# w_in in even and odd partitions, its sums moved to chunk 0, and late query blocks in a home of their own

## The chip, the cores and the metric

The kernel runs on one core of a Trainium2 chip. The metric is the device time of one execution in microseconds; the median of three runs of the kernel before is 273.5 us (273.16 to 273.62). A profiled execution is kept beside it, and every time below is from that one. The engines are PE (matrix products), DVE, ACT and POOL (element by element), and SP, which here only issues transfers (DMA) and transposes by DMA.

## The reference

An attention with a cosine weight feeds a feed-forward layer. Eight batches, eight heads, 576 positions, 64 columns a head; then 4608 tokens of width 512, and a hidden width of 2048.

```python
r = maximum(x, 0); phi(x) = concat([r * cos(theta), r * sin(theta)])     # theta = pi/2 * pos/576
kv  = einsum('bhsf,bhfd', ...)      # phi(k)^T v, one 128 x 64 matrix a head
num = phi(q) @ kv;  den = phi(q) @ sum_s phi(k) + 1e-6
x   = (num / den), heads side by side: 4608 x 512
h   = x @ w_in;  g = h * sigmoid(beta * h);  out = g @ w_out
```

## The kernel before

**Batches and chunks.** A batch has 576 positions; partition p of a head holds positions 9p to 9p+8, so a batch is nine blocks (`NQ`) of 64 positions. Two heads g = 0, 1 lie in partitions 0 to 63 and 64 to 127 of the raw tiles, and index j counts the four pairs. The feed-forward layer works in nine chunks of 512 tokens, eight blocks each, so chunk 0 is blocks 0 to 7 of batch 0, and chunk 1 is block 8 of batch 0 and blocks 0 to 6 of batch 1.

**Attention of a batch.** `load_raw` brings q, k or v (SP's queue; one buffer for each of the three). DVE and ACT take relu of k (`k_relu`, L193/L192) and v times cos and sin (`v_scale`, L219/L217; `vb`). PE multiplies both (`kv_mm`, L276), and ACT or DVE copies the result (`kv_take`, L286). The relu of q (`q_relu`, `qb`) is turned, by PE (`q_turn_pe`, L235, then copies by ACT and tangent products by DVE, L223) in batches 0 and 1, by a DMA transpose (`q_turn_dma`, L259) in the others; the sine half of q is the cosine half times tan (`tan_mul`, `qs`). PE forms the numerators (`num_mm`, L297), DVE divides (`x_rden`, `x_mul`, L308 to L319: `xs`), and `xs` is turned into `xt` by PE (`x_turn_pe`, L356, copied by ACT or DVE, L361/L363) or by DMA (`x_turn_dma`, L367).

**Feed-forward of a chunk.** `h_mm` (L386) multiplies a hidden block of 128 with w_in, `h_act` (L394) applies the silu on ACT. Chunk 0 multiplies g with w_out plainly (`o_mm`, L544). From chunk 1 on the second layer, and from chunk 3 on the first, runs with seven products of halves instead of eight; it needs sums of the operands: of g (`g_sum`, S1 to S4, L406), of x (`x_sum`), of w_in (`wh_sum`, L443, 32 instructions in all) and of w_out (`w_sums`, T1 to T4, L876 to L879).

**Weights.** `load_w` brings w_in in four column blocks and w_out in four row blocks through four stage buffers. w_in's rows come as rows 128j + p, while the attention has its features by (g, jj); so `cast_win` (L111 to L115) writes bf16 with a change of partitions, each instruction on 64 of them. `cast_out` (L121/L123) multiplies w_out by 1/beta. When the stage buffers are free, `wx_tiles` makes four homes of them: two for the sums of w_in, one for x's, one for a second `qs`.

**The order.** All is recorded by hand, engine by engine. Up to the end of chunk 0, 32 slots follow one another: 0 to 15 the hidden blocks, 16 to 31 the second layer; `early` names what is added behind a slot. `rest()` behind slot 4 records the casts of w_in and w_out and the loads of batch 1; `second()` turns q of batch 1 behind slot 23. Chunk 1 has slots 0 to 15 (`h_group`), with `num_rest` (blocks 7 and 8 of batch 1) behind slot 0, `w_sums` behind slot 6 and the kv of batch 2 behind slot 10; then the seven products of the second layer, `x` and `y`, by name ("6" is a product with S2, "cu" ACT's copy of what has come so far). From chunk 2 on `ORDERS` lists the steps of each chunk; in it `W61` is the first sum of w_in's hidden block 12, and so on.

**Start.** The first 58 small products (`warm_pe`) only keep PE busy until data lands. The table of tangents is turned by PE and copied by DVE (L694).

## Time and profile before

| | us |
|---|---|
| median of three runs (lowest, highest) | 273.5 (273.16, 273.62) |
| the profiled execution, its span | 274.44, 272.7 |
| PE, DVE, ACT, POOL busy | 265.3, 224.0, 188.4, 68.3 |
| chunk 0's first complete product group begins | 18.88 |
| second layer of chunk 0 begins | 31.77 |
| chunk 1 begins | 50.36 |
| second layer of chunk 1 begins | 65.91 |
| last matmul ends | 269.0 |

The page gives busy time, and the chain of work that ended last: 85% of the span are PE's, 9% DVE's, 3% a transfer of v. The granted clock of PE is full throughout. The 16 DMA engines are full up to about 44 us (388 GB/s between 20 and 30 us) with the loads of batches 0 and 1 and of all weights. Times of an instruction are counted from the span's start. Where PE waits is read from the table by stretches, and what it waits for from the timelines.

### The profile page before, as it was taken

What the parts mean: (1) busy time and instruction counts of PE and PEld (TensorE: products, weight loads), DVE (VectorE), ACT (ScalarE), POOL (GpSimd) and SP (SyncE); (2) the same over time, 40 slices, a digit from 0 to 9 for tenths busy, and PEclk for the clock granted to TensorE, in tenths of its full rate; (3) what the DMA queues carried; (4) which work ended last, traced back from release to release, by engine and by line L of the source; (5) the groups of instructions that cost most, each with busy time, mean ns of one, the idle gap of its engine ahead of it and who ended that gap; (6) DMA issues with size and microseconds to landing.
All of it is one profiled execution on the core that took longest, in us unless ns stands there. A gap on an engine that the chain in (4) does not pass through costs nothing.

```text
span 272.7 us, 8970 instructions
## 1 busy us (share of the span) xinstructions
PE 265.3 (97%) x3712; PEld 206.8 (76%) x3712; DVE 224.0 (82%) x596; ACT 188.4 (69%) x384; POOL 68.3 (25%) x89
## 2 busy tenths in 40 slices
PE   8899999999899999999999999999999999999994
PEld 8554455455784588888888888888888888888883
DVE  5989969499989889789989997899589768757852
ACT  4778777796419656899489966996696179428920
POOL 1444000510078000660085009300840060000001
PEclk9999999999999999999999999999999999999999
DMA  6999999999969999994589439943600570015005
GB/s 237 374 395 383 392 390 319 379 201 336 284 130 311 240 348 226 240 313 103 147 216 370 92 58 223 332 71 62 181 2 2 61 185 1 2 27 130 0 2 155
DMA packets 50681, 54.00 MB, mean 198 GB/s; under 512 B 31232, under 2 KB 31760, under 8 KB 50640
## 3 DMA queue, kind: packets, MB, share of 16 engines
q1 hardware_dynamic: 47504, 45.55, 59.1%
q0 software_dynamic: 2784, 7.61, 9.6%
q8 instruction: 29, 0.48, 0.7%
q10 hardware_dynamic: 352, 0.27, 0.4%
q14 instruction: 12, 0.10, 0.1%
HBM read 36.71 MB, written 9.44 MB: 169 GB/s over the span
## 4 chain that ended last, share of the span: by engine, by line
PE 85%; DVE 9%; DMA 3%; SPq 1%; issue 1%; ACT 1%; DVEq 0%
PE ps L621 32%; PE ps L511 27%; PE ps L386 10%; PE ps L544 5%; PE ps L563 4%; PE ps L297 3%; DMA raw_v<-in_v_dram 3%; PE ps L276 3%; DVE vb L219 1%; DVE xs L319 1%; DVE qs L223 1%; SPq L79 1%; DVE S L406 1%; DVE rk L193 1%; DVE qb L193 0%
## 5 line engine op out<-in xcount | busy, mean ns | idle before, releaser
L537 POOL DMA_DIRECT2D out_dram<-o_sb x58 | 33.9, 591 | 147.3 <-ACT o_sb L658 86.3
L420 ACT ACTIVATE g_t<-ps,beta 128x512 bf16<-128x512 f32 x96 | 60.3, 702 | 1.4 <-PE ps L511 1.3
L621 PEld LDWEIGHTS <-S 128*128 128x128 bf16 x448 | 43.4, 98 | 5.2
L511 PE MATMUL ps<-w_stage 128*128 128x256 bf16 x288 | 46.6, 272 | 0.1
L386 PE MATMUL ps<-xt,win 128*128 128x512 bf16 (+1 forms) x196 | 42.8, 375 | 0.1
L511 PEld LDWEIGHTS <-w_stage 128*128 128x128 bf16 x384 | 37.3, 98 | 5.1 <-issue 0.2
L487 DVE TENSOR_TENSOR ps<-ps,p 128x256 f32<-128x256 f32 x74 | 30.5, 428 | 8.6 <-PE ps L511 3.0
L394 ACT ACTIVATE g_t<-ps,beta 128x512 bf16<-128x512 f32 x48 | 32.3, 688 | 7.2 <-PE ps L386 7.1
L621 PEld LDWEIGHTS <-g_t 128*128 128x128 bf16 x336 | 32.3, 98 | 4.5 <-ACT g_t L420 0.4
L386 PEld LDWEIGHTS <-win 128*128 128x128 bf16 x196 | 18.7, 98 | 21.1 <-issue 0.5
L511 PE MATMUL ps<-xt,win 128*128 128x256 bf16 x192 | 32.9, 273 | 0.0
L511 PEld LDWEIGHTS <-win 128*128 128x128 bf16 x288 | 28.0, 98 | 3.4
L621 PE MATMUL ps<-wout,g_t 128*128 128x256 bf16 x224 | 28.9, 273 | 0.0
L406 DVE TENSOR_TENSOR S<-g_t 128x512 bf16<-128x512 bf16 (+1 forms) x66 | 25.7, 418 | 3.3 <-ACT g_t L420 1.7
L480 ACT COPY ps<-ps 128x256 f32<-128x256 f32 x62 | 22.6, 383 | 7.5 <-PE ps L621 4.0
L217 ACT ACTIVATE vb<-raw_v,sin 128x256 bf16<-128x256 f32 (+1 forms) x58 | 26.0, 503 | 1.5 <-DMA raw_v<-in_v_dram 1.5
L621 PE MATMUL ps<-T,S 128*128 128x256 bf16 x224 | 26.6, 273 | 0.0
L621 PE MATMUL ps<-wout,S 128*128 128x256 bf16 x224 | 26.4, 273 | 0.0
L319 DVE TENSOR_TENSOR xs<-ps,rden 128x768 bf16<-128x768 f32 (+4 forms) x26 | 22.8, 884 | 0.9 <-DVE rden L312 0.2
L223 POOL TENSOR_TENSOR qs<-qt,tanr 128x1152 bf16<-128x1152 bf16 x6 | 14.3, 2387 | 27.4 <-PE ps L563 21.0
L658 ACT COPY o_sb<-ps 128x512 f32<-128x512 f32 x11 | 6.3, 587 | 20.1 <-PE ps L621 20.1
L487 DVE TENSOR_TENSOR ps<-ps,u 128x256 f32<-128x256 f32 x36 | 15.3, 427 | 5.3 <-PE ps L511 3.3
(112 smaller groups left out, 414.7 us busy)
## 6 DMA issues: line engine op xcount, KB each, us to landing
raw_v<-in_v_dram SPq DMA_DIRECT2D x7, 1152.0 KB, 9.7
raw_k<-in_k_dram SPq DMA_DIRECT2D x7, 1152.0 KB, 9.5
raw_q<-in_q_dram SPq DMA_DIRECT2D x7, 1152.0 KB, 7.4
out_dram<-o_sb POOLq DMA_DIRECT2D x58, 128.0 KB, 4.5
w_stage<-in_moe_w_in_dram SPq DMA_DIRECT2D x3, 1024.0 KB, 12.8
w_stage<-in_moe_w_out_dram SPq DMA_DIRECT2D x2, 1024.0 KB, 7.9
w_stage<-in_moe_w_out_dram SPq DMA_DIRECT2D x4, 512.0 KB, 11.9
out_dram<-o_sb SPq DMA_DIRECT2D x10, 128.0 KB, 2.4
```

The lines of the kernel that those rows point to most:

```text
L217: got = nc.scalar.activation(o, a, AF.Copy, scale=t[:, n : n + 1])
L223: return eng.tensor_tensor(dst.rearrange("q n (g p) -> q n g p", g=2), src.rearrange("q n (g p) -> q n g p", g=2), tanr[:, n0:n1].unsqueez ...
L319: nc.vector.tensor_tensor(o.rearrange("q j n s d -> q j (n s) d"), nv[:, :, a:z, :, 0:D].rearrange("q j n s d -> q j (n s) d"), rden[:, :, ...
L386: nc.tensor.matmul(ps[:, h_bank(c, jt), i * 64 : (i + w) * 64], lhsT=win[jt // 4][:, mi, (jt % 4) * P : (jt % 4 + 1) * P], rhs=xt[:, i : i ...
L394: return nc.scalar.activation(gs[c, jt // 4][:, jt % 4], ps[:, h_bank(c, jt)], AF.Silu, scale=beta[:, jt : jt + 1])
L406: return nc.vector.tensor_tensor(o, l, r, op=op)
L420: return nc.scalar.activation(gs[c, jt // 4][:, jt % 4], bank, AF.Silu, scale=beta[:, jt : jt + 1])
L480: return nc.scalar.copy(at("a", 0), at("b", 0))
L487: nc.vector.tensor_tensor(dst, at("b", 0), st["p5"], op=ALU.add)
L511: nc.tensor.matmul(dst, lhsT=l[:, g], rhs=r[:, :, g * HP : (g + 1) * HP], start=start and g == 0, stop=g == 1, skip_group_check=True)
L537: (eng or own).dma_start(out=out_v[bb, n][:, m0:m1], in_=o_sb[hf * HP : (hf + 1) * HP, m0:m1])
L621: nc.tensor.matmul(dst, lhsT=l(i), rhs=r[:, i], start=start and i == 0, stop=i == order[-1], skip_group_check=True)
```

## The change

**w_in.** Feature column d of head 4 jj + mi now lies at 2d + jj in block mi. The raw tiles keep their pairs but `heads` gives the two heads of a product as j and j + 2; the division writes `xs` with a step of two columns; w_in's rows are loaded so that row d of jj = 0 goes to the even partitions and of jj = 1 to the odd ones, with two transfers of 64 partitions in place of each. `cast_win` then needs no change of partitions: one instruction casts 128 of them.

**Sums.** The 32 sums of w_in go to a home of their own and are taken on DVE in chunk 0 (behind the casts of each column block, and the last of them behind slots 22 and 27). All `W` steps leave `ORDERS`. T1, T2 and T4 are summed in halves, partly in chunk 0; T3 behind slot 0 of chunk 1. S1 to S4 move into two stage buffers.

**Casts.** Blocks 6 and 7 of w_out are cast on ACT, with others changed in place; w_in(0) has four casts (POOL, DVE, ACT, POOL), w_in(1) to (3) four each, all DVE.

**Queries of batch 1.** PE turns blocks 0 to 6. Blocks 7 and 8 get their relu on ACT into a piece of T1, and are turned by two DMA transposes on SP; POOL makes their tangent products. Their numerators (`num_rest`) go behind slot 11 of chunk 1, and the kv of batch 2 with them. Block 8 of batch 0 is multiplied and divided behind slot 22 in place of slot 4; its sine half is kept by a copy of POOL's (`qs_last`).

**Order.** The loads of batch 2 stand behind these transposes on SP; w_out(2) is loaded in two halves around q of batch 1; the relus of q(3) on ACT stand behind the two p copies of the second layer. In chunk 1 the first halves of four hidden blocks come first. Slots 4 to 9 split their products in two of 256 columns.

**Start.** A small read of v stands ahead of beta on ACT's queue, the copies of the table of tangents go to ACT, and four of the first products fall away.

```diff
+    def heads(j0, j1):
+        if j1 - j0 == 4:
+            return slice(0, 4)
+        at = 2 * (j0 % 2) + j0 // 2
+        return slice(at, at + 1) if j1 - j0 == 1 else slice(at, 4, 2)
...
-    w_in_v = moe_w_in.rearrange("(j p) f -> p j f", p=P)
+    late_qb = T1[:, 6:8].rearrange("q i t -> q (i t)").rearrange("q (s n c) -> q s n c", s=2, n=2)
+    w_in_v = moe_w_in.rearrange("(jj mi d) f -> jj d mi f", jj=2, d=HP)
...
-            nc.sync.dma_start(out=st[:, a : a + step], in_=w_in_v[:, a : a + step, i * 512 : (i + 1) * 512])
+            for jj in range(2):
+                nc.sync.dma_start(out=st[jj:P:2, a : a + step],
+                                  in_=w_in_v[jj, :, a : a + step, i * 512 : (i + 1) * 512])
...
+    nc.scalar.dma_start(out=touch, in_=v[0].rearrange("h (s r) d -> (h s) r d", s=2)[:, 0, 0:8])
...
-        parts = ((0, 0, 5), (1, 5, NQ))
+        parts = ((0, 0, 5), (1, 5, NQ)) if b == 0 else ((0, 0, 4), (1, 4, 7))
...
-        o = xs[:, n0:n1, jps[0] : jps[-1] + 1].rearrange("q n s (j d) -> q j n s d", j=2)
+        o = xs[:, n0:n1, jps[0] : jps[-1] + 1].rearrange("q n s (d j) -> q j n s d", j=2)
...
-        nc.vector.tensor_copy(tanr[:, n0:n1, :].rearrange("q n p -> q (n p)"), ps[:, bank, 0 : (n1 - n0) * HP])
+        nc.scalar.copy(tanr[:, n0:n1, :].rearrange("q n p -> q (n p)"), ps[:, bank, 0 : (n1 - n0) * HP])
...
+    def t_sum(kind, i0, i1):
+        o, l, r = {1: (T1, B12, B11), 2: (T2, B22, T1), 4: (T4, B21, T2), 3: (T3, B22, B12)}[kind]
+        nc.vector.tensor_tensor(o[:, i0:i1], l[:, i0:i1], r[:, i0:i1], op=ALU.subtract)
...
     def rest():
+        nc.gpsimd.tensor_copy(qs_last, qs_first[:, :, NQ - 1])
         cast_halves(2)
+        wh_sums(0)
+        wh_sums(2)
         cast_halves(3)
-        x_mul(x_rden(2, 0, 8, NQ, (0, 1)), 8, NQ)
+        wh_sums(4)
+        wh_sums(6)
...
+        load_w("out", 2, 2, 0, 2)
         load_raw(1, "q")
-        load_w("out", 2, 2)
+        load_w("out", 2, 2, 2, 4)
         load_w("out", 3, 2)
-        x_turn_dma(0, 8, 9)
-        for j in range(8):
+        for j in range(4):
             cast_out(j)
+        wh_sums(8)
+        wh_sums(10)
+        cast_out(4)
+        cast_out(5)
+
+    def rest_2():
+        cast_out(6, "a")
+        cast_out(7, "a")
+        v_scale(1, 1, n1=8, eng="act")
+        k_relu(1, 2, 4, "act")
+        t_sum(1, 0, 4)
         v_scale(1, 0)
         v_scale(1, 1, n0=8)
         k_relu(1, 0, 2)
+        t_sum(2, 0, 4)
...
+    def eighth():
+        for jp in range(2):
+            num_mm(0, 8, jp, 4, jp)
+        kv_mm(1, 0, 6)
+        kv_mm(1, 1, 6)
+        kv_take((0, 1), 6, "act")
+        x_mul(x_rden(4, 0, 8, NQ, (0, 1)), 8, NQ)
+        x_turn_dma(0, 8, NQ)
+        cast_out(8)
+        cast_out(9, "a")
+        t_sum(4, 0, 4)
+        wh_sums(12)
+        q_relu(1, 0, n1=7)
+        q_relu(1, 1, n1=4)
+        q_relu(1, 1, "act", 4, 7)
+        for jp in range(2):
+            relu(late_qb[:, jp].rearrange("q n (j d) -> q j n d", j=2), raw_tile(1, "q")[:, jp::2, 7:], "act")
+        for jp in range(2):
+            nc.sync.dma_start(out=qts[1][:, jp, 7:], in_=late_qb[:, jp].rearrange("q n c -> q (n c)"), transpose=True)
+
+    def turn():
+        for jp in range(2):
+            tan_mul(nc.gpsimd, qs_first[:, jp, 7:], qts[1][:, jp, 7:], 7, NQ)
+        load_raw(2, "q")
+        load_raw(2, "v")
+        load_raw(2, "k")
+        takes = [q_turn_pe(1, jp, 4 + 2 * jp, hold=True) for jp in range(2)]
...
+    def sevens():
+        for jp in range(2):
+            num_seven(jp, 4 + 2 * jp)
+        for j in (14, 15):
+            cast_out(j, "a")
+        for jp in range(2):
+            x_mul(x_rden(4 + 2 * jp, 0, 0, 7, (jp,)), 0, 7)
+        t_sum(1, 4, 8)
+        wh_sums(14)
...
-        4: lambda: (num_mm(0, 8, 0, 2, 0), num_mm(0, 8, 1, 2, 1), rest()),
-        15: lambda: (v_scale(1, 1, n1=8, eng="act"), k_relu(1, 2, 4, "act")),
+        4: rest,
+        15: rest_2,
+        22: eighth,
+        25: turn,
+        27: sevens,
+        30: lambda: x_turn_pe(1, 0, 7, 4, ("act",), (0,)),
+        31: lambda: (x_turn_pe(1, 0, 7, 5, ("dve",), (1,))),
...
+    t_sum(2, 4, 8)
+    t_sum(4, 4, 8)
+    for jt in range(4):
+        h_mm(1, jt, (0, 1))
     for slot in range(16):
...
-            num_rest()
             att_q(2)
             v_half(2, 0)
+            t_sum(3, 0, 8)
...
-        elif slot == 10:
+        elif slot == 11:
+            num_rest()
             kv_all(2, eng="act")
+            x_rest()
...
-    q_relu(3, 0, "act")
...
     ops(y, "1 c1")
+    q_relu(3, 0, "act")
+    q_relu(3, 1, "act")
+    q_turn_dma(3)
```

## The prediction

> **What bounds the kernel now.** I read the page first, then the work of each engine by stretches, the chain of waits in order of time, and the timelines of the stretches where the chain leaves PE.
>
> ```profile
> PE 265.3 (97%) x3712; PEld 206.8 (76%) x3712; DVE 224.0 (82%) x596; ACT 188.4 (69%) x384; POOL 68.3 (25%) x89
> ```
>
> PE is busy for all but 7.4 us of the span. The table by stretches says where these are (after the length come PE, PEld, DVE, ACT, POOL, the granted clock, the DMA share and GB/s):
>
> ```profile
> 0.00:10.00 10.00, 8.94 (x106) 7.49 (x106) 6.75 (x21) 5.86 (x10) 2.14 (x11) 1.00 0.79 281
> 10.00:20.00 10.00, 8.45 (x235) 5.06 (x234) 8.99 (x22) 7.23 (x19) 5.62 (x7) 1.00 1.04 387
> 20.00:30.00 10.00, 10.00 (x64) 4.53 (x62) 9.50 (x21) 8.43 (x13) 2.91 (x4) 1.00 1.05 388
> ...
> 60.00:70.00 10.00, 9.18 (x255) 5.91 (x254) 9.86 (x17) 7.47 (x12) 0.00 (x0) 1.00 1.03 338
> 70.00:80.00 10.00, 9.85 (x91) 8.83 (x91) 8.57 (x25) 2.23 (x7) 3.49 (x2) 1.00 0.88 174
> ```
>
> 2.6 us are lost before 20 us, 0.97 us around 70, and 3.7 us behind the last matmul (269.0). Everywhere else PE is full at a granted clock of 1.00. So the change can win only in the head and at 70, or by taking work off PE. The chain shows who held PE at 70:
>
> ```profile
> 51.92 0.18 DVE den L308
> ...
> 59.34 1.14 DVE T L876
> 60.48 0.02 issue
> 60.50 1.24 DVE T L877
> 61.74 0.02 issue
> 61.76 1.23 DVE T L878
> 62.98 1.14 DVE wout L879
> 64.12 2.54 DVE qs L223 x2
> 66.66 2.02 DVE S L406 x6
> 68.68 0.01 issue
> 68.69 1.15 ACT qb L192
> 69.83 0.27 ACT p L602
> ```
>
> DVE works without a pause from 51.92 to 69.26, through the four sums of w_out (T, 4.8 us), the tangent products and the sums S1 and S2. S2 is ready at 69.26. ACT is late as well: it waits for the raw q of batch 3, does its two relus, and only then copies p.
>
> ```profile
> 67.62 2.22 ACT L192 ACTIVATE qb<-raw_q 128x1152 bf16<-128x1152 f32 x2 [0.82 <-DMA raw_q<-in_q_dram]
> 69.74 0.63 ACT L602 COPY p<-ps 128x256 f32<-128x256 f32 x2
> 70.15 1.03 PE L563 MATMUL ps<-T,S 128*128 128x256 bf16 x8 [0.96 <-ACT p L602]
> ```
>
> Both have to go for PE to gain its 0.96 us.
>
> **The stall at 70 (-1.0).** T is now summed in pieces: half of T1, T2 and T4 in chunk 0, the rest of T1 there too; T2 and T4's other halves (0.6 each, half of 1.23) and T3 (1.22) stay in chunk 1. Of DVE's 17.3 us up to the end of S2, 2.4 go. DVE also no longer idles 2.5 us up to 51.92 for the last two query blocks: these move behind slot 11 of chunk 1, and DVE starts chunk 1 when it has copied xt, near 50.6. Without waits it would be through S2 by 65.5; in fact the last g_t comes first. PE reaches its sixth product after 16 groups (13.8), the two blocks (0.5), kv (1.15), two products (1.74) and the numerators (1.34): 50.2 + 18.5 = 68.7 to 69.0. The last silu ends 2.3 us before that, then one S1 piece and four of S2 take 5 x 0.34 = 1.7: S2 is there 0.5 us ahead. The p copies on ACT now stand ahead of the relus of q(3), so the second cause goes too. What hides the rest of DVE's work is this margin, and 1.4 us of slack before S1 (the moved division, 1.05, and the two tangent products, 2.6, follow the two query blocks at 61.3 and end near 65.0).
>
> **PE's own work (-0.24).** Query blocks 7 and 8 of batch 1 turn by DMA. PE transposes 14 blocks where the chain has 18 in 1.07 us: 4 x 0.06 less. Split moving operands in slots 4 to 9 add 18 matmuls of 256 columns for as many columns; the products of that width elsewhere run at the same rate per column (8 in 0.87 us against 4 of 512 in 0.86), so nothing. Four warm-up matmuls fewer lie in a head that waits for data.
>
> **The head (-0.1).** w_in(0) is cast in four instructions, one on DVE, where eight were, two on DVE:
>
> ```profile
> 15.65 1.18 DVE L115 CAST win<-w_stage 64x512 bf16<-64x512 f32 x2
> 16.86 0.17 DVE L308 TENSOR_TENSOR den<-ps,eps 128x14 f32<-128x14 f32 x1
> ```
>
> The second took 0.72. Without it the division waits for its matmuls, which end at 16.72: 0.1 us won, not 0.7. The cast of all 128 partitions has the same 512 elements in each, so I keep the 0.42. The strided writes of xs are shown by no row; the two divisions behind it take 1.14 us out of PSUM, and I take 0, with another 1.1 us (twice that) as the bad end. Moving the tan copies to ACT (0.45 each) frees DVE of 0.85 us ahead of 12.2, where raw_v lands and sets the pace; ACT is idle there until 6.69. The small read of v is ahead of beta on ACT's queue, and costs one issue (0.45) before the first table load, hidden by the same landing. What it does to v's transfer no row shows: 0, with -0.6 (DMA at 281 GB/s in the first stretch against 387) and +0.45 as ends.
>
> **w_in's transfers (0).** Each becomes two of 64 partitions, the even and the odd. One MB lands every 2.7 us (w_in 2 and 3 at 21.87 and 24.56), which is the 388 GB/s of the whole queue, and the 512 KB loads of w_out keep that rate too. I take no loss.
> The Trainium skill speaks against it: "DMA: Bandwidth & Descriptors", Rules for kernel authors, says of two transfers to disjoint partition halves not to bother and to use one of 128, and "SBUF — State Buffer", Door 1, measures 196 GB/s for partitions 0 to 63 against 328 for all: by that w_in would take 1.7 times as long (an estimate from that page), a milder form of a rival below. The same section derives the port from the bits above the lowest two, by which every second partition still reaches all ports; no run here has shown that.
>
> **Chunk 0 on DVE and ACT (+0.1).** The queue is full until 44, so landings stay: w_in 19.1, 21.9, 24.6, w_out 27.3 and 30.0, v 33.2, k 36.2, then the first half of w_out(2) 37.5, q 40.5, the second half 41.9. DVE has 12 casts where it had 20 (0.49 each) but takes 24 sums of w_in by slot 15 (four take 0.93 in chunk 1's end, 75.27 to 76.19). In order: w_in(1) done 21.1, w_in(2) 23.8, eight sums 25.7, w_in(3) 27.6 (first quarter 26.2; PE wants it at 28.0), eight sums 29.5, w_out 0 to 3 31.1 (PE 31.6), eight sums and w_out 4 and 5 33.8 (PE 35.1; 6 and 7 on ACT 33.6, where v's landing would hold it until 33.2 anyway), T1 34.4, v 37.0, k 37.8 (PE's kv 37.9), half T2, the division, w_out 8 39.5 (PE 39.9), half T4, four sums, q 42.0 (PE's turn 41.7), w_out 10 42.5 (PE 42.8). POOL keeps two casts of nine, which shortens DVE's (0.72 to 0.83 beside POOL's, 0.42 alone), and takes a copy and two small tangent products that nobody waits for before 60. The second half of T1 must wait until the late turns have read their home in it; behind it on DVE stands the second copy of xt (50.0), which half of chunk 1's first products need. DVE gets there at 48.2, the turns end near 47 (next part), so 0, and at their late end 2 us more. The margins are thin; one is missed by 0.3, and the wait at 44.5 for a q copy (0.2) goes. I take +0.1, between -0.2 and +0.9.
>
> **SP's queue (+0.1).** The loads of batch 2 stand behind three DMA transposes now.
>
> ```profile
> 34.30 2.68 SPq L367 DMA_TRANSPOSE xt<-xs  x1
> 40.40 0.38 SPq L79 DMA_DIRECT2D raw_q<-in_q_dram  x1
> 40.83 0.56 SPq L79 DMA_DIRECT2D raw_v<-in_v_dram  x1
> ```
>
> v landed 11.5 us after its issue, at 52.3, and ACT and DVE use it at 54.2. After: the turn of block 8 is issued near 39; the late turns wait for ACT's relus of q (40.5 plus three and a cast, 42.2), each costs SP 0.5 (73.42 has three of six blocks in 5.4 with waits) to 2.7 us; the loads follow at 43.3 to 47.6 instead of 40.4. The queue was full of w_out until 44 anyway, so v lands at 53.3 to 57, middle 54.4. ACT takes it behind the silu of slot 2, at 54.2; behind it wait the silus, and for these PE's banks, with 0.4 us in hand at slots 7 to 10. 0.1 lost, up to 2.6 at the late end.
>
> **Sum.** Chunks 2 to 8 lose their 24 sums on DVE, where PE waits for nothing: 0. -1.0 - 0.24 - 0.1 + 0.1 + 0.1 = -1.1. The profiled execution took 274.44 (span 272.7), so 273.3 there; the median of the runs is 273.5, 0.9 less, and gives 272.4. Two terms lean downward (the wait at 44.5, the read of v), so I say 272.3.
>
> **Rivals.** (1) Slower: v of batch 2 comes too late. If the late turns cost SP 2.7 each, v lands at 57; ACT stands from 54.2, slot 7 (due 56.2) gets its bank at 58.2, and ACT's four pairs of silu and scale (1.1 against PE's 0.86) add 0.5: 2.6 where the forecast has 0.1, 274.8. It decides from a landing of about 56 on (no gain left). For: a 2.68 and a 2.28 for small turns stand in the trace. Against: both fell on a full queue, and 34.30's queue was longer. 0.18. (2) The gain at 70 goes to a new wait: the turn of q(2) lands after 63.5, or raw_q(3) holds ACT's u copies; half of the 1.0 comes back, 273.0 to 273.5. For: k(2) is ahead of that turn. Against: it no longer has the turn of four blocks (2.28) before it. 0.14. (3) w_in's pairs take twice the time: w_in(3) at 35 where PE wants it at 28, and all behind it: 280 to 284. 0.05.  (4) The head gains 0.5 more because v lands earlier: 271.7. 0.1. The rest, 0.53, is the forecast.
>
> **Numbers.** 0.2% (0.55 us) is what a measurement of this kernel can tell. Faster: 0.53 less a little for thin margins, plus 0.1: 0.6. Same: (2), 0.14. Slower: (1), (3) and missed margins, 0.26. The range leaves out (3) and the far end of (1): 271.4 (all good ends of the head) to 274.3.
>
> **What would show it.** Right: no idle time of PE before its sixth product in chunk 1, T in chunk 0's rows, PE's chunk 1 begun near 50.1, end of the last matmul near 267.9. Wrong: waits of ACT or DVE for raw_v or raw_k between 53 and 60, of PE for ACT's g_t; POOL's or DVE's first w_in cast after 15.7; PE waiting for w_out or kv between 31 and 43.

## Result: 276.0 us, 1.0% slower, and the profile after

The changed kernel takes 276.0 us (median of four runs, 275.19 to 277.43) against 273.42 for the kernel before: a ratio of 1.010, 95% interval 1.0058 to 1.0143. The forecast was 272.3, faster. The profiled execution is the fastest of the four, 275.19 with a span of 273.4; the other three are 0.8 to 2.2 us longer, and no trace shows them. Here and below, a run over 1.5% longer than the fastest of its kernel is left out of the ratio (two of `c_late_st`, two of `d_late_behind`, one of `f_a_nocols`, and one of the kernel before, 1532.68 us).

The page's row for PE, and the table by stretches (columns as before: length, PE, PEld, DVE, ACT, POOL, granted clock, DMA share, GB/s):

```profile
PE 265.7 (97%) x3719; PEld 208.5 (76%) x3722; DVE 219.5 (80%) x586; ACT 189.7 (69%) x390; POOL 65.1 (24%) x85
```

```profile
0.00:10.00 10.00, 8.32 (x100) 7.25 (x101) 5.51 (x19) 5.96 (x11) 2.91 (x11) 1.00 0.83 294
10.00:20.00 10.00, 9.21 (x235) 5.23 (x234) 8.19 (x21) 7.67 (x20) 3.10 (x5) 1.00 1.04 381
20.00:30.00 10.00, 10.00 (x68) 6.38 (x67) 8.70 (x32) 8.40 (x14) 0.00 (x0) 1.00 1.05 386
...
60.00:70.00 10.00, 9.25 (x284) 6.09 (x284) 6.59 (x16) 5.30 (x10) 0.00 (x0) 1.00 1.10 289
70.00:80.00 10.00, 9.88 (x89) 8.33 (x89) 8.88 (x24) 3.45 (x7) 0.99 (x1) 1.00 1.20 251
```

The stretch from 60 to 70 should have been full. PE still loses 0.75 us there. DVE, which worked 9.86 of these 10 us before, now works 6.59: it was relieved as planned, and waits. The chain in order of time says for what:

```profile
49.71 3.39 PE ps L398 x16
53.10 12.07 DMA qt<-qb
65.26 2.63 DVE qs L232 x2
67.89 2.68 DVE w_stage L418 x8
70.94 1.03 DVE xs L331
72.02 8.89 PE ps L574 x80
```

Chunk 1 begins at 49.71, as forecast and better. Then the chain leaves the engines for 12 us: the DMA transpose of q(2), issued at 53.10, lands at 65.2. Behind it stand the tangent products, the sums S1 and S2 and the division, and PE waits in small pieces from 67.2 to 72.0. The rows of DVE, PE and ACT (in brackets the idle time before an instruction, and what ended it):

```profile
65.26 2.63 DVE L232 TENSOR_TENSOR qs<-qt,tanr 128x1152 bf16<-128x1152 bf16 x2 [3.34 <-DMA qt<-qb]
67.94 0.23 PE L308 MATMUL ps<-kv,qs 64*64 64x65 bf16 x4 [0.55 <-DVE qs L232]
69.58 2.22 ACT L200 ACTIVATE qb<-raw_q 128x1152 bf16<-128x1152 f32 x2 [2.00 <-DMA raw_q<-in_q_dram]
```

SP's queue shows why the turn is late:

```profile
41.18 3.11 SPq L833 DMA_TRANSPOSE qt<-T  x2
44.39 0.53 SPq L86 DMA_DIRECT2D raw_q<-in_q_dram  x1
...
53.10 7.08 SPq L268 DMA_TRANSPOSE qt<-qb  x1
```

The two late turns of batch 1 hold SP from 41.18 to 44.29, and the loads of batch 2 start 4.0 us later than before (40.40). The turn of q(2) is issued 2.4 us earlier than before (55.47), but takes 7.08 us to issue where it took 4.65. From the list of issues (median us from issue to landing) in the stretch from 54 to 65, first the kernel before, then the changed one:

```profile
qt<-qb SPq DMA_TRANSPOSE x1, 6.7
```

```profile
qt<-qb SPq DMA_TRANSPOSE x1, 12.1
```

In that stretch the DMA engines have three things to carry: the last packets of k(2), which lands at 58.1 (before at 55.3), the turn, and the eight stores of chunk 0, which POOL issues. The stores meet the turn in the kernel before as well, 0.6 MB of them from 55 on, but there they are through by 59; in the changed kernel 0.3 MB of them still run beside the turn from 60 to 65. A second place is late too: at 108.1 PE waits 0.32 us for a result of DVE, which stands behind its work on a v issued at 96.44, before at 93.74 (DVE waited 0.98 us for it, ACT 2.90).

### The profile page after: what moved, and what is told of

It reads as the page before. It is cut to its first block, busy times and chain, and to the rows that moved or that the text cites. A ratio compares the mean times of both kernels' runs of the same rounds, so it can differ in the third digit from the quotient of the medians.

```text
span 273.4 us, 8999 instructions
## 1 busy us (share of the span) xinstructions
PE 265.7 (97%) x3719; PEld 208.5 (76%) x3722; DVE 219.5 (80%) x586; ACT 189.7 (69%) x390; POOL 65.1 (24%) x85
## 4 chain that ended last, share of the span: by engine, by line
PE 84%; DMA 8%; DVE 5%; ACT 1%; issue 1%; ACTq 0%; DVEq 0%
PE ps L632 28%; PE ps L522 27%; PE ps L398 11%; PE ps L555 5%; DMA qt<-qb 4%; DMA raw_v<-in_v_dram 4%; PE ps L308 3%; PE ps L574 3%; PE ps L285 3%; PE ps L244 1%; DVE w_stage L418 1%; DVE qs L232 1%; PE ps L690 1%; DVE xs L331 1%; DVE vb L228 1%
## 5 line engine op out<-in xcount | busy, mean ns | idle before, releaser
L632 PEld LDWEIGHTS <-w_stage 128*128 128x128 bf16 x448 | 43.4, 98 | 5.2
L522 PE MATMUL ps<-w_stage,ws 128*128 128x256 bf16 x288 | 46.5, 272 | 0.1
L522 PEld LDWEIGHTS <-ws 128*128 128x128 bf16 x384 | 37.3, 98 | 5.3 <-issue 0.5
L398 PEld LDWEIGHTS <-win 128*128 128x128 bf16 x214 | 20.7, 98 | 19.4
L522 PEld LDWEIGHTS <-win 128*128 128x128 bf16 x288 | 28.0, 98 | 3.4
L232 POOL TENSOR_TENSOR qs<-qt,tanr 128x1152 bf16<-128x1152 bf16 (+1 forms) x8 | 15.6, 1965 | 58.5 <-DMA qt<-T 27.9
L418 DVE TENSOR_TENSOR w_stage<-g_t 128x512 bf16<-128x512 bf16 (+1 forms) x66 | 25.8, 421 | 2.9 <-ACT g_t L432 1.5
L632 PE MATMUL ps<-T,w_stage 128*128 128x256 bf16 x224 | 26.6, 273 | 0.0
L632 PE MATMUL ps<-wout,w_stage 128*128 128x256 bf16 x224 | 26.4, 273 | 0.0
L331 DVE TENSOR_TENSOR xs<-ps,rden 128x768 bf16<-128x768 f32 (+4 forms) x26 | 24.3, 943 | 0.9 <-DVE rden L324 0.2
L228 DVE TENSOR_SCALAR vb<-raw_v,cos 128x256 bf16<-128x256 f32 x63 | 21.6, 393 | 1.7 <-DMA raw_v<-in_v_dram 1.7
```

Source lines behind the costliest of these rows:

```text
L228: got = nc.vector.tensor_scalar(o, a, scalar1=t[:, n : n + 1], scalar2=None, op0=ALU.mult)
L331: nc.vector.tensor_tensor(o.rearrange("q j n s d -> q j (n s) d"), nv[:, :, a:z, :, 0:D].rearrange("q j n s d -> q j (n s) d"), rden[:, :, ...
L398: nc.tensor.matmul(ps[:, h_bank(c, jt), i * 64 : (i + w) * 64], lhsT=win[jt // 4][:, mi, (jt % 4) * P : (jt % 4 + 1) * P], rhs=xt[:, i : i ...
L418: return nc.vector.tensor_tensor(o, l, r, op=op)
L522: nc.tensor.matmul(dst, lhsT=l[:, g], rhs=r[:, :, g * HP : (g + 1) * HP], start=start and g == 0, stop=g == 1, skip_group_check=True)
L632: nc.tensor.matmul(dst, lhsT=l(i), rhs=r[:, i], start=start and i == 0, stop=i == order[-1], skip_group_check=True)
```

## Experiments

Seven theories are named in the expectations. **L**: the late turns stand ahead of the loads of batch 2, which end later and push the turn of q(2) into the stores. **W**: w_in's pairs of transfers or the first 50 us lose the time. **M**: the stall at 70 belonged to the one profiled execution of before. **O**: the order on SP behind 60 us. **Q**, **R**: stores or late turns cost the queue their time wherever they stand. **I**: PE waits for its own code.

To compare traces I take the time at which PE has a given number of matmul columns still to do, and subtract the same time in an execution of the kernel before that took 273.48 us (`c_before2`). Some matmul records are missing, so a tenth is noise. The heads give that execution's times.

| us later (+) or earlier (-) | 47.3 | 64.5 | 72.4 | 110.5 | 172.5 | end |
|---|---|---|---|---|---|---|
| before, as profiled for the prediction | +0.1 | +0.1 | +1.0 | +1.0 | +1.0 | +1.0 |
| changed kernel | -0.7 | -0.6 | +1.1 | +1.6 | +1.6 | +1.8 |
| changed, again (`a_ctrl`) | -0.1 | +0.1 | +1.7 | +1.8 | +1.9 | +2.1 |
| before + two late turns (`b_twoturns`) | +0.4 | +0.5 | +1.6 | +2.3 | +2.1 | +2.3 |
| changed, no late turns (`a_peturn`) | -0.1 | -0.3 | -0.3 | +1.2 | +2.1 | +2.1 |
| changed, no stores of chunk 0 (`a_nostore0`) | -0.2 | -0.3 | -0.3 | -0.3 | -0.4 | -0.4 |
| before, no stores of chunk 0 (`d_b_nostore0`) | -0.2 | -0.2 | -0.2 | -0.2 | -0.4 | -0.5 |
| `a_peturn` + old order (`c_pe_rest0`) | -0.3 | -0.1 | 0.0 | 0.0 | +0.8 | +0.8 |
| before + w_in part (`d_win_only`) | -0.5 | -0.5 | +0.2 | +0.2 | 0.0 | +1.4 |
| before + split operands (`f_b_cols`) | +0.2 | +0.2 | +0.2 | +0.2 | +1.3 | +1.4 |
| changed, operands not split (`f_a_nocols`) | -0.5 | -0.2 | +2.8 | +2.8 | +2.8 | +2.9 |

**1. The changed kernel again (`a_ctrl`, no edit).**

> The changed kernel as it is, for the spread of its times and a second profile. Theory L (the two late turns stand ahead of the loads of batch 2, these end 3 us later, run into the stores of chunk 0, and the turn of q(2) lands at 65 where before it landed at 62): 275 to 277.5 us again, with the tangent products of batch 2 on DVE begun at 65 or later, and later in a slower execution. Theory W (w_in's pairs or another part of the first 50 us lose the time): the same time, but chunk 1 begun later than 50.5 us in a slower execution.

276.08 (eight runs, 274.28 to 277.55), ratio 1.0086, interval 1.0056 to 1.0115, with the same waits at 67 to 73. The scatter is the kernel's own.

**2. No late turns (`a_peturn`): PE turns all nine blocks of batch 1.**

```diff
-        parts = ((0, 0, 5), (1, 5, NQ)) if b == 0 else ((0, 0, 4), (1, 4, 7))
+        parts = ((0, 0, 5), (1, 5, NQ))
...
-        q_relu(1, 0, n1=7)
-        q_relu(1, 1, n1=4)
-        q_relu(1, 1, "act", 4, 7)
-        for jp in range(2):
-            relu(late_qb[:, jp]..., raw_tile(1, "q")[:, jp::2, 7:], "act")
-        for jp in range(2):
-            nc.sync.dma_start(out=qts[1][:, jp, 7:], in_=late_qb[:, jp]..., transpose=True)
+        q_relu(1, 0)
+        q_relu(1, 1, n1=5)
+        q_relu(1, 1, "act", 5)
...
-            tan_mul(nc.gpsimd, qs_first[:, jp, 7:], qts[1][:, jp, 7:], 7, NQ)
```

> The changed kernel with all nine query blocks of batch 1 turned by PE again; no late turn on SP. Theory L: the loads of batch 2 are issued at 42 and not 44.4 to 45.5, k(2) lands before 56, the turn of q(2) by 62.5, DVE's tangent products begin by 63, no wait of PE before the sixth product; PE has 0.24 us more; 272.3 to 273.0 us. Theory W: within 0.5 us of the changed kernel, 275.5 to 276.5.

275.19 (274.9 to 275.75), ratio 1.0058, interval 1.0036 to 1.0079: 0.9 of the 2.6 us come back. The stall at 70 is gone, as L says, and PE is ahead of the kernel before at 72.4. But it stops at 79:

```profile
62.42 3.42 SPq L379 DMA_TRANSPOSE xt<-xs  x1
69.95 5.04 SPq L268 DMA_TRANSPOSE qt<-qb  x1
...
80.84 0.38 PE L398 MATMUL ps<-xt,win 128*128 128x512 bf16 x1 [1.39 <-DMA xt<-xs]
```

The last two blocks' turn, which the change moved behind slot 11, now stands behind the loads of batch 3, and the turn of q(3) and the x of chunk 2 behind it. Another 1.1 us goes at 155, for no reason that an engine's rows show.

**3. No stores of chunk 0 (`a_nostore0`, and its counterpart on the kernel before, `d_b_nostore0`).** `store` returns at once for chunk 0, so these rows of the output stay unwritten.

> The changed kernel without the eight stores of chunk 0 (its 512 rows of the output are left out). Theory L, by collision with the stores: k(2) ends 1 us earlier, the turn of q(2) takes 7 us and not 12 and lands at 61 to 62, the waits before the sixth product go, 273 to 274 us. If the turn is late only because k(2) is ahead of it: it lands at 63 to 64 and 1 us of the loss stays. Theory W: no change, 275.5 to 276.5.

> The kernel before without chunk 0's eight stores (its output lacks these rows). It is the counterpart to the changed kernel without them, which took 273.53. Theory L (only the changed kernel's turn of q(2) meets the stores at a price): 273.1 to 273.5, under 0.15% faster. Rival S (any kernel of this form gains from 1 MB less): 271.5 to 272.5.

273.53, ratio 0.9992 (0.9977 to 1.0007): the whole loss is gone. The kernel before gains nothing by it (273.77, ratio 1.0007, 0.9994 to 1.002). So the stores cost only the changed kernel, where the turn of q(2) is issued before k(2) has ended and the stores drag on beside it. The turn and the stretch without them:

```profile
53.60 4.15 SPq L268 DMA_TRANSPOSE qt<-qb  x1
```

```profile
60.00:70.00 10.00, 10.00 (x296) 6.93 (x295) 8.99 (x22) 7.92 (x14) 0.00 (x0) 1.00 1.05 371
```

4.15 us of issue in place of 7.08, a landing after 7.6 in place of 12.1, and PE full. The turn lands at 61.2 although k(2) is nearly as late as in the changed kernel (57.7 for 58.1), so the late k(2) alone does not make the loss. And even with the collision gone, the changed kernel is no faster than the one before.

**4. Late turns put into the kernel before (`b_twoturns`): two transposes of qb's last blocks into unused room, ahead of the loads of batch 2.**

```diff
         if slot == 24:
+            spare = T4[:, 6:8]...
+            for jp in range(2):
+                nc.sync.dma_start(out=spare[:, jp], in_=qb[:, jp, 7:]..., transpose=True)
             for name in "qvk":
                 load_raw(2, name)
```

> The kernel before with two additional DMA transposes of query blocks 7 and 8 (into a spare piece of T4, read by nobody) ahead of the loads of batch 2 on SP; no arithmetic is changed. Theory L: the loads end 2 to 3 us later, the turn of q(2) lands at 64.5 or later where DVE wants it at 64.0; 0.5 to 2 us slower, 274 to 275.5. Theory W: within 0.3 us of before.

274.5 (273.87 to 276.1), ratio 1.0037, interval 1.0018 to 1.0057. Two transposes that nobody waits for cost 1.0 us, and in the trace, which is of its longest run (276.1), the waits are where the changed kernel has them (0.35 at 69.8, 0.51 at 108.6). The loads start 3.4 us later than before:

```profile
40.40 3.28 SPq L871 DMA_TRANSPOSE T<-qb  x2
43.77 0.53 SPq L79 DMA_DIRECT2D raw_q<-in_q_dram  x1
```

**5. The kernel before, profiled again (`c_before2`).**

> The kernel before, profiled a second time. The profiled execution that the prediction was worked out from took 274.44 us, 0.96 above the median of the kernel before (273.48). Theory M (the stall of PE at 70 belongs to that one execution): this profile shows a time near 273.4, no idle of PE of over 0.3 us ahead of the sixth product at 70, and the products of chunk 2 begin about 1 us earlier than 80.8; then 1.0 us of the predicted gain was never there in the median run. Rival N (the stall is in every execution): idle of about 1 us at 70 again, whatever the time.

273.48, and no stall. Two rows of its table, ACT's relus of q(3) with the copies behind them, and PE's sixth product:

```profile
60.00:70.00 10.00, 9.97 (x263) 6.68 (x261) 9.86 (x17) 7.65 (x12) 0.00 (x0) 1.00 1.04 352
70.00:80.00 10.00, 10.00 (x92) 8.82 (x91) 9.40 (x26) 2.00 (x6) 3.56 (x2) 1.00 0.84 140
```

```profile
66.62 2.21 ACT L192 ACTIVATE qb<-raw_q 128x1152 bf16<-128x1152 f32 x2
68.73 0.63 ACT L602 COPY p<-ps 128x256 f32<-128x256 f32 x2
69.14 1.91 PE L563 MATMUL ps<-T,S 128*128 128x256 bf16 x16
```

ACT starts the relus 1.0 us earlier than in the first profile (67.62, after waiting 0.82 for raw_q), and the sixth product follows the numerators within 0.2 us. DVE is as busy as ever, 9.86 of 10, and S2 comes as late (ready at 69.18, in the first profile at 69.26); it did not hold PE. What differs is SP's queue: in the first profile the turn of x at 53.08 held it for 2.28 us and q(3) was issued at 60.21, here for 1.21 us and at 59.26. Theory M holds for these two executions: the one that the prediction was made from was 0.96 us above the median, and its stall at 70 is that 0.96. A few runs of the kernel before are as long (five of the 26 beside `a_ctrl` took 274.05 or more); no trace shows what holds them.

**6. The stores moved behind the turn, on SP (`c_late_st`; with the next edit, `c_pe_rest0_st`).**

```diff
     def store(c, tt, o_sb, m0=0, m1=DM, eng=None):
...
+            if c == 0:
+                held_stores.append((out_v[bb, n], o_sb, hf))
+                continue
...
     def att_q(b, turn=True):
...
             q_turn_dma(b)
+        while held_stores:
+            o_, sb_, hf = held_stores.pop(0)
+            nc.sync.dma_start(out=o_, in_=sb_[hf * HP : (hf + 1) * HP])
```

> The changed kernel with the eight stores of chunk 0 issued on SP right behind the turn of q(2), instead of on GpSimd as soon as their copies are done. Theory L (the late turns move the loads of batch 2, and these push the turn of q(2) into the stores of chunk 0): the turn of q(2) takes about 4.2 us of issue as in the kernel without these stores (7.1 in the changed kernel), the wait of DVE for it (3.3 us) shrinks below 1.5, PE has no waits of over 0.2 us between 66 and 73, and the time is 273.5 to 274.3. Rival Q (the bytes are in the way wherever they stand: the loads of batch 3 then come 2 to 3 us later and a later turn or load is late instead): 275 to 276, with the waits moved to 79 or later.

> The kernel of the run before this one with, besides, the stores of chunk 0 issued on SP behind the turn of q(2). Theories L and O together: 272.6 to 273.4, as fast as the kernel before or faster, no wait of PE of over 0.3 us between 60 and 112. Rival Q: the loads of batch 3 come later by the stores' 2.7 us (1.05 MB at 388 GB/s) and k or v of batch 3 or the turn of q(3) is late: 274 to 275.

279.58 (ratio 1.0189, 1.015 to 1.0227) and 279.4 (1.0226, 1.0185 to 1.0268). The turn then takes 4.13 us, as L says, but the eight stores hold SP for 5.6 us, the loads of batch 3 start at 63.0, and xt of chunk 2 is late. What follows is worse than the wait itself (the trace of `c_late_st` is of a run of 281.07):

```profile
84.33 1.89 PE L398 MATMUL ps<-xt,win 128*128 128x512 bf16 x4 [2.75 <-DMA xt<-xs]
```

```profile
84.00:90.00 6.00, 5.67 (x14) 2.10 (x15) 6.00 (x14) 2.11 (x4) 6.00 (x8) 0.50 0.96 313
```

After this idle of 2.75 us, and one of 1.53 before it that ends at 80.5, the granted clock is 0.50 for the next 6 us. `c_pe_rest0_st` (a run of 280.07) has an idle of 2.83 us for xt at 80.8, and 0.57 from 84 to 88. Both theories missed the time, rival Q by 3.6 us and more, but the waits moved to 79 and later as Q said: behind the turn this megabyte is in the way too, and at a higher price.

**7. The late turns behind the loads (`d_late_behind`): the second halves of the T sums go back behind slot 6, where the home of the late blocks is free.**

> The changed kernel with the two late turns of batch 1 issued on SP behind the three loads of batch 2 instead of ahead of them; the late halves of the T sums stand where the kernel before had its sums (behind the sixth group of chunk 1), since the home of the late blocks lies in T1. Theory L (the place of the late turns ahead of the loads is what the change loses at 70): loads of batch 2 issued near 41.5 instead of 44.4, the turn of q(2) landed by 63, no waits of PE of over 0.2 us at 67 to 73, 273.0 to 274.0. Rival R (the late turns cost the queue the same time wherever they stand): the turn of q(2) lands after 64.5, 275 to 276.

276.07 (273.67 to 280.71), ratio 1.0066 (1.0039 to 1.0093): as slow as the changed kernel. The only trace is of its longest run, 280.71, so little but the queue is read from it:

```profile
43.44 5.50 SPq L839 DMA_TRANSPOSE qt<-T  x2
52.03 6.73 SPq L268 DMA_TRANSPOSE qt<-qb  x1
...
66.75 2.63 DVE L232 TENSOR_TENSOR qs<-qt,tanr 128x1152 bf16<-128x1152 bf16 x2 [1.94 <-DMA qt<-qb]
```

The loads start at 41.76 and the turn of q(2) lands no earlier. The time is rival R's, and the queue of this one long run agrees: it is the late turns, not only their place ahead of the loads.

**8. The old order behind 60 us (`c_pe_rest0`): `a_peturn` with the last two blocks' numerators, division and turn at slot 0 of chunk 1 again.**

> The changed kernel with all nine blocks of batch 1 turned on PE (no late turns) and, besides, the last two blocks' products of batch 1 with their division and their turn at the start of chunk 1, ahead of the turn of q(2), as in the kernel before. Theory O (the wait of 1.55 us for the turned x at 79 comes from the queue: the turn of those two blocks stands behind the loads of batch 3 and pushes the turn of q(3) and the three turns of batch 2 back): no wait of PE at 79, turn of q(3) ends near 73.5 as before, 273.4 to 274.2. Rival: the wait at 79 comes from something else (DVE's later sums), it stays, 275.2 as without this edit.

The wait at 79 is gone, and PE runs level with the kernel before up to 150 us: O holds there. But the time is 275.02 (ratio 1.0056, 1.0042 to 1.0069), 0.8 above what was expected. In the trace, of its shortest run (274.34), what is left is the idle at 154, here the PE rows:

```profile
152.38 1.69 PE L632 MATMUL ps<-T,w_stage 128*128 128x256 bf16 x14
155.00 0.38 PE L632 MATMUL ps<-T,w_stage 128*128 128x256 bf16 x2 [0.93 <-issue]
155.22 1.04 PE L632 MATMUL ps<-wout,g_t 128*128 128x256 bf16 x8
```

PE stops in the middle of a product with S4, whose operands are all there.

**9. Is it PE's code? 16 instructions more at the start (`d_pe_rest0_w`).** `warm_pe(62, 48)` for `warm_pe(54, 48)`, else as in 8.

> The kernel with all nine blocks turned on PE and the rest's turn ahead of the turn of q(2) (275.02 us, with an idle of PE of 1.09 us at 153.8 that no other engine's work explains), with 62 warm-up products at the start instead of 54. They lie in a stretch where PE waits for the table of tangents anyway (0.89 us at 3.1), so they should cost under 0.1 us by themselves. Theory I (the idle at 154 hangs on where PE's code is cut into loaded blocks, since it is seen only in the kernels with this instruction count): it goes or moves, 273.8 to 274.4. Rival (something in the work at 154): it stays at 1.1, 275.0.

274.93 (274.71 to 275.07), the rival's time: the edit wins nothing. The idle is still there, but elsewhere in the work, as theory I allowed:

```profile
152.93 0.82 PE L632 MATMUL ps<-T,w_stage 128*128 128x256 bf16 x6
154.71 1.25 PE L632 MATMUL ps<-T,w_stage 128*128 128x256 bf16 x10 [0.97 <-DVE rden L324]
155.80 0.93 PE L632 MATMUL ps<-wout,g_t 128*128 128x256 bf16 x7
```

6 matmuls of S4 come before it and 10 behind it, where it was 14 and 2: exactly the 8 matmuls and 8 weight loads that were put in. (`rden` is no operand of these matmuls; it is only the last thing that ended before.) The idle sits at a count of PE's instructions, not at a piece of work. The changed kernel's page counts the loads of code:

```profile
q8 instruction: 29, 0.48, 0.8%
```

29 loads for PE's 3719 + 3722 instructions are one for 257, of 0.48 MB / 29, some 16 KB each.

**10. The same warm-up in half as many products of twice the width, 54 to 58 PE instructions fewer and no column changed (`e_b_warm`, `e_win_warm`, `e_a_warm`, `e_pe_rest0_warm`).**

```diff
-    warm_pe(58, 48)
+    warm_pe(29, 96)
```

> The kernel before with the same edit of the warm-up only (29 products of 96 columns for 58 of 48). No other engine's work changes. Theory I: the time may move by up to 1.2 us for each block boundary that falls shortly behind a burst of small products, with a new idle without releaser in the trace: 273.3 to 275.5, and if it moves at all, by such an idle. Rival (code is never waited for): 273.3 to 273.7 and no such idle.

> The kernel before with the w_in part alone, and PE's 58 warm-up products of 48 columns written as 29 of 96: the same columns, 58 PE instructions fewer. Theory I (the two idles of PE of that kernel, 0.81 us at 68.2 and 1.20 at 179.1, are PE waiting for code, and hang on where the 256-instruction blocks fall): both go or shrink below 0.3, 273.3 to 274.2. Rival W (the strided writes or the pairs of transfers cost 1.9 us in the time, code or not): 275.2 to 275.7 again, with the idles at the same work.

> The changed kernel with 27 warm-up products of 96 columns for 54 of 48. Theory L (its loss is the turn of q(2) beside the stores, a matter of SP's queue): the waits of PE at 67 to 73 stay, 275.4 to 276.4. Theory I as the main cause of the change's loss: 274 or less.

> The kernel with all nine blocks turned on PE and the rest's turn ahead of the turn of q(2) (275.02, idle of 1.09 at 154), with 27 warm-up products of 96 columns for 54 of 48. Theory I: the block boundary now falls 54 instructions, some 3 us of products, farther behind the burst of small products at 150.6, the code is there in time, no idle at 154: 273.7 to 274.2. Rival: something in the work at 154, 274.9 to 275.1 and the idle again.

| | as it was | warm-up in half as many | ratio to before (95%) |
|---|---|---|---|
| kernel before | 273.5 | 285.54 | 1.0438 (1.041 to 1.0466) |
| before + w_in part | 275.47 | 283.55 | 1.0361 (1.0335 to 1.0388) |
| changed kernel | 276.0 | 280.79 | 1.0256 (1.0222 to 1.029) |
| `c_pe_rest0` | 275.02 | 279.92 | 1.0227 (1.019 to 1.0264) |

All four expectations missed, by 4 us and more. In three of them theory I foretold a shorter time; it rose. For the kernel before it foretold a loss of at most 2 us, and 12 came. The warm-up itself takes 2.50 us with 29 products as with 58, and the granted clock is 1.00 behind it, so neither its length nor its clock is the reason. What was not foreseen is how many other boundaries would fall badly. From the kernel before with this edit:

```profile
17.59 0.23 PE L356 MATMUL ps<-ident,xs 128*128 128x128 bf16 x1 [2.15 <-issue]
76.33 1.03 PE L563 MATMUL ps<-T,S 128*128 128x256 bf16 x4 [3.90 <-DVE rden L312]
```

```profile
17.50:22.00 4.50, 4.41 (x81) 2.53 (x82) 3.08 (x10) 1.92 (x5) 0.55 (x1) 0.62 1.05 389
70.00:80.00 10.00, 6.10 (x175) 4.78 (x174) 7.79 (x22) 3.37 (x7) 0.00 (x0) 0.83 1.20 270
```

PE stands still for 2.15 us at 15.4 and 3.90 at 72.4, and each time runs at a lower granted clock behind it (0.62 and 0.83 on the average of these stretches). The list of DMA queues has one load of code between 73.8 and 75.0, and none from 70 to 73.8 or from 75 to 77:

```profile
q8 instruction: 1, 0.02, 5.4%
```

S2 and the p copies were done by 72.7; the load takes from 73.85 to 74.89, and PE goes on 1.44 us later. The burst ahead of the stop, from 71.0 to 72.4, has 144 products and as many weight loads, more than one load's worth in 1.4 us. In this trace PE ends 11.1 us later than in `c_before2`; its five stops without a releaser (2.15, 0.35, 3.90, 1.38 and 0.61) are 8.4 of them, and the lower clock took some 3 more (an estimate: 4.5 us at 0.62 and 10 at 0.83 are 1.7 us each).

The Trainium skill, "Runtime: NRT & Kernel Launch", Instruction fetch mechanics, describes such blocks of 16 KiB or 256 instructions, which the sequencer fetches over a DMA queue of its own. The count above agrees. It calls the cost of crossing a block boundary mostly hidden; here it is 0.6 to 3.9 us where a load comes late, and the measurement decides.

**11. The split operands of slots 4 to 9, 36 PE instructions: taken out of the changed kernel (`f_a_nocols`), put into the kernel before (`f_b_cols`).**

```diff
-            h_group(0, slot, 2 if slot < 10 else 1)
+            h_group(0, slot)
```

> The changed kernel without the split of moving operands in slots 4 to 9 (18 matmuls and their weight loads fewer, the same columns). Theory I (the place of the bursts of small products among PE's blocks of code decides, and the split is what puts them right in the changed kernel): idles of PE with no releaser appear behind bursts, 277 to 282. Rival, as the prediction had it (a split costs and gives nothing): 275.4 to 276.6, the same waits as in the changed kernel.

> The kernel before with the split of moving operands in slots 4 to 9 and nothing else of the change (18 matmuls and their weight loads more, the same columns). Theory I: all later block boundaries fall 36 instructions earlier in the work, code is late behind a burst at 68 or later, 274.5 to 280. Rival: 273.3 to 273.7.

Without the split the changed kernel takes 279.33 (ratio to before 1.0175, 1.0136 to 1.0215); with it the kernel before takes 274.73 (1.0024, 1.0006 to 1.0043). The idles, first of the changed kernel without it, then of the kernel before with it:

```profile
71.64 0.22 PE L308 MATMUL ps<-kv,qs 64*64 64x65 bf16 x2 [2.53 <-issue]
```

```profile
154.47 0.70 PE L621 MATMUL ps<-T,S 128*128 128x256 bf16 x5 [0.83 <-issue]
```

Theory I holds for both: the same columns, and 3.3 us more or 1.1 us more. But the trace without the split is of the shortest run, 276.37; the other five are 2.9 to 4.2 us longer, at a granted clock of 0.992 to 0.994, and no trace shows where.

**12. The w_in part alone (`d_win_only`): the kernel before with the order of heads, the pairs of transfers, the casts over 128 partitions and the strided xs.**

> The kernel before with only the w_in part of the change: the order of heads, w_in in even and odd partitions by pairs of transfers, casts over 128 partitions (all on VectorE from the second quarter of w_in on), x written at a stride of two elements; nothing else of the change. The prediction gave this part about 0: theory L expects 273.2 to 273.8. Rival W (the pairs of transfers or the strided writes cost something): 274.3 or more, with chunk 0 begun later than 20 us or PE waits at the x transposes.

275.47 (ratio 1.0064, 1.0045 to 1.0082): 1.9 us slower, against L's expectation. Not by W either: chunk 0 begins on time, and at 64.5 PE is 0.5 us ahead. It then loses 0.7 at 68 and 1.3 at 179, in bursts of small products whose operands are there:

```profile
68.98 0.22 PE L304 MATMUL ps<-kv,qs 64*64 64x65 bf16 x2 [0.64 <-issue]
180.36 0.23 PE L304 MATMUL ps<-kv,w_stage 64*64 64x65 bf16 x4 [1.03 <-issue]
```

PE's stream is that of the kernel before, but it reaches the first burst half a microsecond sooner. The run that should have shown that this is late code (`e_win_warm`) brought larger idles. The place of the stops shows it instead. Below are the stops of over 0.6 us whose operands were there, by the number of PE's instructions (matmuls and weight loads) in the trace ahead of them; a few records are missing.

| instructions ahead | stops there, us |
|---|---|
| 450 | `e_b_warm` 2.15, `e_win_warm` 2.23, `e_a_warm` 1.91, `e_pe_rest0_warm` 0.69 |
| 1983 to 1986 | `d_win_only` 0.64, `d_late_behind` 0.98, `f_a_nocols` 2.53, `e_b_warm` 3.90, `e_win_warm` 2.95, `e_a_warm` 2.62, `e_pe_rest0_warm` 3.15 |
| 2753 | `e_b_warm` 1.38, `e_win_warm` 1.46 |
| 4541 to 4545 | `a_peturn` 0.98, `c_pe_rest0` 0.93, `d_pe_rest0_w` 0.97, `f_b_cols` 0.83 |
| 5313 | `d_win_only` 1.03, `e_b_warm` 0.61, `e_win_warm` 0.64 |

Eleven kernels with different work in these places stop behind the same five numbers, which lie multiples of 256 apart to within a few records, and PE goes on 1.2 to 1.6 us after a load of code has landed (2.1 in the second stop of `d_win_only`, whose load took 3.1 us). So the stops of `d_win_only` and the one of `a_peturn` at 155 are code as well. The traces of the changed kernel and of the kernel before have no such stop.

No version tried beats the kernel before.

## Why the prediction was wrong

**The stall at 70 (-1.0).** Its mechanism in the profiled execution may stand: raw_q(3) came late, ACT's p copies with it. Its size in the measured time was 0. The failed step is the sum: it set out from 274.44, took off the stall of 0.97, and then took off another 0.9 to come to the median. `c_before2`, a single second profile, shows that these were the same microsecond. From 273.5, without that term, the same sum gives 273.4, "no change". DVE's share in the stall was misread: S2 was ready at 69.18 in the run without it, at 69.26 in the run with it. So "both have to go" was wrong, and relieving DVE could not win the 1.0.

**SP's queue (+0.1) and rival (2).** The second failed step, and the one that makes the kernel slower. The two late turns held SP for 3.11 us, inside the 1.0 to 5.4 given, and v came in time (ACT took it at 53.81; DVE at 53.75, after waiting 0.72 us for it), so rival (1) did not come true. What was not followed was the queue itself: k(2), behind v, lands at 58.1 where it landed at 55.3, and the turn of q(2) behind k shares the DMA engines with it and with stores that run on to 65. Rival (2) named this turn and its limit of 63.5; it landed at 65.2. Its price, half of 1.0, had only the gain at stake; without that gain to lose, what came of the late loads cost 1.7 us of PE's progress between 64.5 and 72.4 and 0.5 more at 108. Against it stood that the turn of four blocks no longer came before it. True, and worth less than the stores that it now met.

**PE's own work (-0.24).** Neither confirmed nor refuted: with the stores left out of both, the changed kernel takes 273.53 and the kernel before 273.77, but the intervals overlap, and the other small terms are in this difference too; that it is just 0.24 is luck. "Split moving operands ... nothing" is wrong in kind. The columns are the same, and the instructions are not: without the split the changed kernel loses another 3.3 us. The sum had no term for where PE's code is cut. In its two traces the changed kernel pays nothing for that, by luck and not by design; most of its variants do.

**The head (-0.1), chunk 0 (+0.1).** Chunk 0's first complete product group begins at 18.93 (18.88 before), so the head won nothing. The casts and sums in chunk 0 held: PE lost 0.21 us between 30 and 40 and 0.05 between 40 and 50, `c_before2` 0.21 and 0.26. Chunk 1 began 0.65 us earlier than before (49.71 for 50.36), but `a_ctrl` was only 0.1 us ahead at 47. The division at a stride of two took 1.02 us for 0.96 (128x768), off the path.

**w_in's transfers (0), rival (3).** Right for the transfers: 381 to 386 GB/s between 10 and 30 us, 387 to 388 before. Of the Trainium skill, "SBUF — State Buffer", Door 1, derives the port from bits above the lowest two, and the rate here agrees; its 196 GB/s for partitions 0 to 63, and a loss of the kind that "DMA: Bandwidth & Descriptors", Rules for kernel authors, warns of for disjoint halves, were not seen with every second partition. That the w_in part by itself still cost 1.9 us (experiment 12) came from PE's code, not from its transfers.

**What stays open.** The runs of the changed kernel scatter over 3 us, and the traces show two of them, 275.19 and 275.55; what makes the longer ones longer is not known. Why the stores, which the kernel before clears by 59, drag on to 65 in the changed one is seen only as far as they compete with k(2) and the turn. Late code is shown as the reason of the stops; no run shows a way to keep all of them out.

## What to carry to other kernels

Before a stall in a profile is counted as a gain, set the profiled execution against the median: a stall of the size of that difference may not be in the median at all, and a second profile settles it. The price of a small transfer put ahead of large ones is paid by whoever stands last behind them, even when the next in line comes in time; follow the queue to its next idle stretch and price the turn that then meets other traffic. In a kernel that keeps PE 97% busy, an edit that changes the number of PE's instructions, even in a warm-up, moves all later work against the boundaries between blocks of code. Look for idles of PE without a releaser, count PE's instructions up to them, and try a few counts before judging the edit.

## What the runs showed of the hardware that was not expected

- PE's code comes in loads of some 16 KB, one for 257 instructions, listed among the DMA queues beside the data. Late loads, most of them behind a burst of small products, stopped PE for 0.6 to 3.9 us, always at the same counts of its instructions, and PE went on 1.2 to 1.6 us after the load had landed (74.89 and 76.33 in `e_b_warm`; once 2.1).
- 58 instructions fewer in the head, at equal columns, cost the kernel before 12 us (273.5 to 285.5).
- Idles of PE of 2.15 us, and of 1.53 and 2.75 shortly after one another, were followed by a granted clock of 0.62 over 4.5 us and of 0.50 over 6 us. Idles of 0.6 to 1.4 us were not, and neither was every longer one: behind the 2.53 us of `f_a_nocols` it stayed at 1.00.
- A DMA transpose of 18 blocks landed 7.6 us after its issue without the stores beside it and 12.1 us with them, when the stores ran on to 65; in the kernel before, where they were through by 59, it landed after 6.7.
